# Keys of a 448-token attention in chunks of 3 x 128 + 64 instead of 4 x 112, in a fused attention and two-layer kernel

## Chip, cores and metric

The kernel runs on one core of one Trainium2 chip. The metric is the device time of one execution in microseconds; the time before is the median of three runs.

## What is computed

There are 8 batches of 12 heads with 448 tokens of 64 elements. The attention has a sigmoid in place of a softmax; behind it stand two matrix products with h - tanh(h) between them. The weights arrive as 64-bit floats.

```python
scores = matmul(q, k.transpose(0, 1, 3, 2)) / sqrt(64) - log(448)
attn = 1.0 / (1.0 + exp(-scores))
x = matmul(attn, v).transpose(0, 2, 1, 3).reshape(8 * 448, 768)
h = x @ w_in              # w_in 768 x 2048
g = h - tanh(h)
out = g @ w_out           # w_out 2048 x 768
```

## The kernel before, in words

Two heads make a pair, six pairs a batch. The transposed K and Q of a pair lie with head 0 in partitions 0 to 63 and head 1 in 64 to 127. Keys are worked off in four chunks of `CK` = 112. A chunk's scores (`scores`, L357) are matmuls with K as the weights, 64 rows and 112 columns of TensorE's array for each head, so that the heads use the two halves of its rows; each writes its own PSUM bank of the tile `sc`. Then ACT takes the sigmoid of both heads in one instruction of 112 x 896 (`weigh`, L376). AV (`av`, L386) has V's 64 columns as the weights and 112 rows, so that the heads use the two halves of the array's columns and write the two halves of the partitions of one bank, `acc`.

From batch 2 on (`AV32` = 2) everything runs in pairs of fp16 numbers, a high and a low part, and three products stand for one: six matmuls per chunk and pair for the scores, six for AV. The attention weights are split by ACT and DVE (`split_a`, L382 and L383, tile `ahl`), V by DVE (`prep_v`). Batch 1 has split scores and fp32 AV (`av32`). Batch 0 is fp32 throughout (`attention32`), its K and Q transposed by TensorE.

Tokens are loaded as `(p c)`: partition p holds tokens 4p to 4p+3, chunk c is the tokens that are c modulo 4. Each of K and Q comes in one DMA per head, V of both heads in one. For batches 1 to 7 the split K and Q (tile `w`, one buffer) are transposed by a DMA that SP issues (L343). `norms` squares K, Q and V on ACT (L308) for the scale factors. The stores of the second layer (`store` in `moe2`) undo the order of tokens, and cut a tile of 128 tokens in two where it crosses a chunk.

The stream of attention work (`stream`, pairs g = 0 to 41 of batches 1 to 7) is cut into 84 blocks of two chunks each: the first of a pair has chunks 0 and 1, the AV of the whole pair before and the next loads; the second has chunks 2 and 3 and the `norms` three pairs ahead. Seven preparing steps run within the first layer of batch 0, four blocks in `first`, and the rest within the second layer (`moe2`) of the batch before, at steps that tables set (`BLOCKS0` with 9 blocks, `BLOCKS1` with 14, `BLOCKS` with 12; 48 steps and a remainder per batch, one step being one slice f of the hidden units). The order on TensorE (PE), ACT, DVE and POOL is the order in which the code is written; only SP's order of DMAs is set by the scheduler.

During the attention of batch 0 the weights w_in come in as 24 `raw` pieces (`conv_load`, L131), are turned from 64 to 32 bits on ACT and DVE (L146 to L168), and share the queue of SP with K, Q and V. After them come the 32 `rawo` pieces of w_out, between which the stream's first loads stand.

Of the kernel before, what the change touches and what calls it, by code (L numbers as in the profile page):

```python
# [34 lines left out]
class Builder:  # L35
# [266 lines left out]
    def norms(self, loaded):  # L302

        n = len(loaded)
        ss = self.sm.tile([CK, 3], F32, name="ss", bufs=3)
        for i, t in enumerate(loaded):
            junk = self.sm.tile([CK, 8 * D], BF16, name="sqn", tag="sq", bufs=4)
            self.nc.scalar.activation(junk, t.rearrange("p a b d -> p (a b d)"), AF.Square, accum_out=ss[:, i : i + 1])  # L308
        return ss[:, :n]

    def scales(self, ss):
# [3 lines left out]
        pb = self.ps.tile([P, 512], F32, name="pbn", tag="tr", bufs=1)[:, :n]  # L315
        nc.tensor.matmul(pb, self.onesf[:CK, :], ss, start=True, stop=True)
        t = self.sm.tile([P, 3], F32, name="tn")
# [30 lines left out]
    def prep_v(self, vn, s):  # L348
        nc = self.nc
        flat = vn.rearrange("p h c d -> p (h c d)")  # L350
        v = self.att.tile([CK, 2, 2, 4, D], F16, name="vhl", tag="vhl", bufs=3)
        vf = v.rearrange("p x h c d -> p x (h c d)")
        nc.vector.tensor_scalar(vf[:, 0], flat, s[:CK, 2:3], None, op0=ALU.mult)
        nc.vector.scalar_tensor_tensor(vf[:, 1], flat, s[:CK, 2:3], vf[:, 0], op0=ALU.mult, op1=ALU.subtract)
        return v

    def scores(self, c, K, Q):  # L357

        nc = self.nc
        S = self.S  # L360
        cs = slice(c * CK, (c + 1) * CK)
# [10 lines left out]
    def weigh(self, ps, scale):  # L372
        nc = self.nc
        S = self.S
        a = self.tp.tile([CK, 2, S], F32, name="a32", tag="t")
        nc.scalar.activation(a, ps[:CK, :, :S], AF.Sigmoid, bias=self.nls[:CK], scale=scale)  # L376
        return a

    def split_a(self, a):
        nc = self.nc  # L380
        A = self.tp.tile([CK, 2, 2, self.S], F16, name="ahl", tag="t")
        nc.scalar.activation(A[:, 0], a, AF.Copy, scale=A_SCALE)  # L382
        nc.vector.scalar_tensor_tensor(A[:, 1], a, A_SCALE, A[:, 0], op0=ALU.mult, op1=ALU.subtract)  # L383
        return A

    def av(self, c, acc, v, A):  # L386
        nc = self.nc
        prods = ((0, 0), (1, 0), (0, 1))
# [10 lines left out]
    def av32(self, c, acc, vn, a):  # L399
        for h in range(2):  # L400
            self.nc.tensor.matmul(
                acc[h * D : (h + 1) * D, : self.S], vn[:, h, c, :], a[:, h], start=(c == 0), stop=(c == 3)
            )

# [29 lines left out]
    def stream(self):  # L434
# [33 lines left out]
        def prep_v(g):  # L468
            if g >= G:
                return  # L470
            if splits(g):
                vv[g] = self.prep_v(v.pop(g), sc[g][0])
            else:
                vv[g] = self.load_v(*at(g), self.att, "vhl", 3)

# [18 lines left out]
        def do_av():  # L494
            for g, c, A in todo:
                if c == 0:
                    self.acc = self.ps.tile([P, 512], F32, name="acc", tag="av", bufs=1)
                    if g % NP == 0:
                        self.xs = []
                (self.av if splits(g) else self.av32)(c, self.acc, vv[g], A)  # L500
                if c == 3:
# [5 lines left out]
        for g in range(G):  # L507
            for i in range(2):
                if i:
                    scales(g + 2)  # L510
                pss = [self.scores(c, K[g], Q[g]) for c in (2 * i, 2 * i + 1)]
                aa = [self.weigh(pss[0], sc[g][1][:CK, 0:1])]
                if i:
                    parts_k(g + 2)
                elif g:
                    parts_q(g + 1)
                aa.append(self.weigh(pss[1], sc[g][1][:CK, 0:1]))
                if i == 0 or not splits(g):
# [16 lines left out]
    def attention32(self, b, weights, rest):  # L535
# [14 lines left out]
        def prep(j):  # L550
            out = []
            for n, name in ((0, "K"), (1, "Q")):
# [4 lines left out]
                else:  # L557
                    nc.vector.tensor_copy(o, t)
                out.append(o)
            return out  # L560

        def av():
            j, c, a = todo.pop(0)
            if c == 0:
                self.acc = self.ps.tile([P, 512], F32, name="acc", tag="mm", bufs=2)
            self.av32(c, self.acc, loaded[j][2], a)
            if c == 3:
                xs.append(self.evac_x(j, self.acc, None))
# [4 lines left out]
        for j in range(NP):  # L573
            for c in range(4):
                ps = self.ps.tile([P, 2, 512], F32, name="sc", tag="sc", bufs=2)
                for h in range(2):
                    r = slice(h * D, (h + 1) * D)
                    nc.tensor.matmul(
                        ps[:CK, h, :S], qk[j][0][r, c * CK : (c + 1) * CK], qk[j][1][r], start=True, stop=True
                    )  # L580
                todo.append((j, c, self.weigh(ps, 1.0 / math.sqrt(D))))
                if j == 0 and c < 2:
# [187 lines left out]
    def moe2(self, b, gs):  # L770
# [6 lines left out]
        base = b * S  # L777
        rows = self.out[base : base + S].rearrange("(p c) e -> p c e", c=4)
        prods = ((0, 0), (0, 1), (1, 0))
        last = (self.NF - 1, 2)  # L780

        def store(o, j0, n, cols):

            i = 0
            while i < n:
                c, p = divmod(j0 + i, CK)
                k = min(n - i, CK - p)
                nc.sync.dma_start(rows[p : p + k, c, cols], o[i : i + k])
                i += k

# [57 lines left out]
    def build(self):  # L848
# [138 lines left out]
```

## Time and profile before

| what | value |
|---|---|
| runs | 1244.72 us median, 1244.56 to 1246.42 |
| profiled execution, span from first to last instruction | 1247.9 us |
| PE busy, matmuls | 1202.3 us, x7675 |
| DVE busy / ACT busy | 941.6 / 942.0 us |
| DMA | 89.76 MB, 192317 packets |

Of the profiled execution the page gives the span alone, no time of its own beside it; the span lies above all three runs. The tenths of busy time in 40 slices show PE at 9 in nearly every slice behind the ninth (a slice is 31 us), and at 7 to 9 before; the granted clock is 9 tenths or more throughout. A wait is put down to the instruction that came last, and idle time of an engine other than PE costs nothing by itself.

### The profile page before, as it was taken

The numbers are of one execution on the slowest core, as the hardware profiler recorded it, in microseconds if no ns is written. First come the engines' busy times: TensorE is split into PE (matmuls) and PEld (weight loads), VectorE is DVE, ScalarE is ACT, GpSimd is POOL, SyncE is SP. The second block draws the span as 40 slices with busy tenths as digits, with TensorE's granted clock in tenths as the row PEclk, the third lists the DMA queues.
The fourth block names the chain that finished last, engine by engine and source line by source line (L and its number), as shares of the span: only waits on it lengthen the run. The fifth ranks groups of instructions, "written<-read, shape, count | busy, mean of one in ns | idle before, by whom it ended". The sixth has DMA issues, their size and how long they took to land.

```text
span 1247.9 us, 19830 instructions
## 1 busy us (share of the span) xinstructions
PE 1202.3 (96%) x7675; PEld 651.9 (52%) x7675; DVE 941.6 (75%) x1473; ACT 942.0 (75%) x1325; POOL 38.0 (3%) x38
## 2 busy tenths in 40 slices
PE   9889887999999999999999999999999999999998
PEld 3235433455555555555555555555555655555555
DVE  4879987888966798668976789668985789636930
ACT  5857796967998688886888788886888877864820
POOL 0100000000000000100001000000000000000000
PEclk9999989999999999999999999999999999999999
DMA  9963358220044400432034400552024410300001
GB/s 241 282 171 83 89 124 208 64 61 8 4 111 100 92 1 13 107 93 57 1 65 108 95 2 1 102 110 57 1 55 100 89 25 1 72 21 20 1 14 32
DMA packets 192317, 89.76 MB, mean 72 GB/s; under 512 B 169824, under 2 KB 182368, under 8 KB 192224
## 3 DMA queue, kind: packets, MB, share of 16 engines
q1 hardware_dynamic: 191296, 88.28, 30.4%
q8 instruction: 60, 0.98, 0.3%
q10 hardware_dynamic: 928, 0.23, 0.1%
q14 instruction: 33, 0.27, 0.1%
HBM read 58.20 MB, written 11.01 MB: 55 GB/s over the span
## 4 chain that ended last, share of the span: by engine, by line
PE 71%; DVE 11%; ACT 10%; DMA 4%; issue 3%; SPq 1%; DVEq 0%; ACTq 0%
PE ph L674 31%; PE po L796 22%; PE sc L367 6%; PE acc L391 5%; PE por L834 5%; DMA raw<-moe_w_in 2%; ACT a L376 2%; ACT ahl L382 1%; ACT sqn L308 1%; DVE ahl L383 1%; DVE m L748 1%; DVE m L762 1%; DVE m L759 1%; DVE g L659 1%; DMA K<-w 1%
## 5 line engine op out<-in xcount | busy, mean ns | idle before, releaser
L796 PE MATMUL po<-wo,g 128*128 128x384 f16 x2304 | 394.1, 327 | 7.5 <-DVE o L826 4.9
L674 PE MATMUL ph<-xhl,wi 128*128 128x448 f16 x2016 | 382.6, 352 | 0.0
L796 PEld LDWEIGHTS <-g 128*128 128x128 f16 x2304 | 220.1, 98 | 183.5 <-issue 43.4
L674 PEld LDWEIGHTS <-wi 128*128 128x128 f16 x2016 | 196.7, 98 | 185.0 <-issue 1.8
L383 DVE SCALAR_TENSOR_TENSOR ahl<-a,ahl 112x896 f16<-112x896 f32 x144 | 155.7, 1122 | 68.6 <-ACT ahl L382 68.5
L376 ACT ACTIVATE a<-sc,nls,rn 112x896 f32<-112x896 f32 x168 | 179.5, 1092 | 18.7 <-PE sc L367 18.2
L744 ACT ACTIVATE u<-ph,ih 128x896 f32<-128x896 f32 x64 | 64.4, 1006 | 91.6 <-PE ph L674 87.9
L382 ACT ACTIVATE ahl<-a 112x896 f16<-112x896 f32 x144 | 128.3, 941 | 0.1
L367 PE MATMUL sc<-Q,K 64*112 64x448 f16 x1008 | 116.2, 361 | 8.9 <-ACT a L376 7.3
L748 DVE SCALAR_TENSOR_TENSOR m<-ph,ihk,u 128x896 f32<-128x896 f32 x64 | 73.4, 1147 | 38.0 <-ACT th L746 37.7
L658 ACT ACTIVATE g<-m,Sg 128x896 f16<-128x896 f32 x64 | 66.7, 1042 | 32.7 <-DVE m L762 27.3
L391 PE MATMUL acc<-ahl,vhl 112*64 112x448 f16 x864 | 89.0, 355 | 0.8 <-DVE ahl L383 0.8
L367 PEld LDWEIGHTS <-K 64*112 64x112 f16 x1008 | 60.9, 128 | 47.5 <-issue 27.8
L341 DVE SCALAR_TENSOR_TENSOR w<-qn,sn,w 112x512 f16<-112x512 f32 x42 | 31.5, 750 | 70.5 <-ACT w L338 70.2
L762 DVE COPY_PREDICATED m<-u,th 128x896 f32<-128x896 uint32 x64 | 77.3, 1208 | 6.6
L659 DVE SCALAR_TENSOR_TENSOR g<-m,Sg,g 128x896 f16<-128x896 f32 x64 | 73.3, 1146 | 8.5 <-ACT g L658 8.4
L704 PE MATMUL ph<-x,wi 128*128 128x448 f32 x192 | 76.5, 549 | 0.0
L759 DVE SCALAR_TENSOR_TENSOR m<-q,m 128x896 f32<-128x896 f32 x64 | 70.0, 1093 | 8.3 <-ACT q L758 1.2
L749 DVE SCALAR_TENSOR_TENSOR th<-ph,ih,th 128x896 f32<-128x896 f32 x64 | 73.2, 1143 | 0.0
L761 ACT ACTIVATE u<-u,b 128x896 f32<-128x896 f32 x64 | 66.8, 1044 | 6.4 <-DVE m L748 4.4
L755 DVE SCALAR_TENSOR_TENSOR m<-q,m 128x896 f32<-128x896 f32 x64 | 69.5, 1086 | 0.0
L391 PEld LDWEIGHTS <-vhl 112*64 112x64 f16 x864 | 46.0, 110 | 40.6 <-issue 13.4
(130 smaller groups left out, 1236.3 us busy)
## 6 DMA issues: line engine op xcount, KB each, us to landing
raw<-moe_w_in SPq DMA_DIRECT2D x24, 512.0 KB, 8.3
rawo<-moe_w_out SPq DMA_DIRECT2D x32, 384.0 KB, 4.1
kn<-k SPq DMA_DIRECT2D x96, 112.0 KB, 2.8
vn<-v SPq DMA_DIRECT2D x48, 224.0 KB, 3.1
qn<-q SPq DMA_DIRECT2D x94, 112.0 KB, 2.9
out<-o SPq DMA_DIRECT2D x7, 336.0 KB, 2.7
out<-o SPq DMA_DIRECT2D x7, 288.0 KB, 2.7
out<-o SPq DMA_DIRECT2D x7, 240.0 KB, 3.2
```

Of the source, the lines that this page charges most:

```text
L367: nc.tensor.matmul(ps[:CK, h, :S], K[r, w, cs], Q[r, x, :], start=(n == 0), stop=(n == len(prods) - 1))
L376: nc.scalar.activation(a, ps[:CK, :, :S], AF.Sigmoid, bias=self.nls[:CK], scale=scale)
L382: nc.scalar.activation(A[:, 0], a, AF.Copy, scale=A_SCALE)
L383: nc.vector.scalar_tensor_tensor(A[:, 1], a, A_SCALE, A[:, 0], op0=ALU.mult, op1=ALU.subtract)
L391: nc.tensor.matmul(acc[h * D : (h + 1) * D, : self.S], v[:, w, h, c, :], A[:, x, h], start=(c == 0 and n == 0), stop=(c == 3 and n == 2),)
L659: nc.vector.scalar_tensor_tensor(g[:, 1], m, Sg, g[:, 0], op0=ALU.mult, op1=ALU.subtract)
L674: nc.tensor.matmul(ph[:, e, :S], self.wi[:, c * self.NB + k, part, e * P : (e + 1) * P], xhl[c][:, x, :], start=(i == 0), stop=(i == 3 * s ...
L704: nc.tensor.matmul(ph[:, e, :S], self.where("in", c)[:, f * P : (f + 1) * P], xs[c], start=(c == 0), stop=(c == self.NC - 1),)
L748: V.scalar_tensor_tensor(m, ps, ihk, u, op0=ALU.mult, op1=ALU.mult)
L759: V.scalar_tensor_tensor(m, q2, C2, m, op0=ALU.add, op1=ALU.mult)
L762: V.copy_predicated(m, u.bitcast(U32), th)
L796: nc.tensor.matmul(po[i][:, :H], gs[f // 2][:, x, f % 2, tk * P : (tk + 1) * P], self.wo[:, i * self.NF + f, w], start=(f == 0 and n == 0) ...
```

## The change

Tokens are loaded in natural order, `(c p)`. K and Q keep their tiles of 112 partitions (and so the transposes), but the transposed columns are now tokens 0 to 447 in order, and the keys are cut into three chunks of 128 and one of 64. For the last chunk head 0 uses rows 0 to 63 and columns 0 to 63 of the array, head 1 rows 64 to 127 and columns 64 to 127. Both heads' scores of it lie in one bank, in the two halves of the partitions, so that the sigmoid and the split of the last chunk work on 128 x 448 instead of 112 x 896. V is a tile of 128 partitions and 7 rows of 64: three chunks for each head, and the seventh with head 0's last 64 tokens in the lower half and head 1's in the upper. It comes in four DMAs instead of one. The sums of squares lie in three fixed tiles that are zeroed once, since K and Q fill 112 rows of them and V 128. Each store is one DMA. `av32` is gone into `av`, and batch 0 uses the same `scores`.

```diff
-                queue.dma_start(t[:, :, h, :], src[b, 2 * j + h].rearrange("(p c) d -> p c d", c=4))
+                queue.dma_start(t[:, :, h, :], src[b, 2 * j + h].rearrange("(c p) d -> p c d", c=4))
...
     def load_v(self, b, j, pool, tag, bufs):
-        t = pool.tile([CK, 2, 4, D], F32, name="vn", tag=tag, bufs=bufs)
-        self.nc.sync.dma_start(t, self.v[b, 2 * j : 2 * j + 2].rearrange("h (p c) d -> p h c d", c=4))
+        t = pool.tile([P, 2 * QT + 1, D], F32, name="vn", tag=tag, bufs=bufs)
+        for h in range(2):
+            src = self.v[b, 2 * j + h]
+            self.nc.sync.dma_start(
+                t[:, h * QT : (h + 1) * QT], src[: QT * P].rearrange("(c p) d -> p c d", c=QT)
+            )
+            self.nc.sync.dma_start(t[h * D : (h + 1) * D, 2 * QT], src[QT * P :])
         return t
...
     def scores(self, c, K, Q):
...
-        prods = ((0, 0), (0, 1), (1, 0))
+        prods = ((0, 0), (0, 1), (1, 0)) if K.dtype == F16 else ((0, 0),)
         for n, (w, x) in enumerate(prods):
             for h in range(2):
                 r = slice(h * D, (h + 1) * D)
+                o = ps[:, h, : self.S] if c < QT else ps[r, 0, : self.S]
                 nc.tensor.matmul(
-                    ps[:CK, h, :S], K[r, w, cs], Q[r, x, :], start=(n == 0), stop=(n == len(prods) - 1)
+                    o,
+                    K[r, w, c * P : min((c + 1) * P, self.S)],
+                    Q[r, x, :],
+                    start=(n == 0),
+                    stop=(n == len(prods) - 1),
                 )
...
+    def weigh(self, c, ps, scale):
+        n = 2 if c < QT else 1
+        a = self.tp.tile([P, 2, self.S], F32, name="a32", tag="t")[:, :n]
+        self.nc.scalar.activation(a, ps[:, :n, : self.S], AF.Sigmoid, bias=self.nls, scale=scale)
...
+        n = a.shape[1]
+        A = self.tp.tile([P, 2, 2, self.S], F16, name="ahl", tag="t")[:, :, :n]
...
     def av(self, c, acc, v, A):
...
             for h in range(2):
-                nc.tensor.matmul(
-                    acc[h * D : (h + 1) * D, : self.S],
-                    v[:, w, h, c, :],
-                    A[:, x, h],
+                o = slice(h * D, (h + 1) * D)
+                k, j, i = (slice(0, P), h * QT + c, h) if c < QT else (o, 2 * QT, 0)
+                self.nc.tensor.matmul(
+                    acc[o, : self.S],
+                    v[k, w, j],
+                    A[k, x, i],
                     start=(c == 0 and n == 0),
-                    stop=(c == 3 and n == 2),
+                    stop=(c == QT and n == len(prods) - 1),
                 )
...
-                nc.sync.dma_start(rows[p : p + k, c, cols], o[i : i + k])
-                i += k
+            nc.sync.dma_start(self.out[base + j0 : base + j0 + n, cols], o)
...
+        self.sums = [const(f"ss{i}", 0.0, 3) for i in range(3)]
```

The written order on PE, ACT, DVE and POOL stays; shapes change in it. The first place is ACT in the second block of a pair (chunks 2 and 3) of a batch with split AV: `a` are the sigmoids, `ahl` the halves, `sqn` the squares of `norms`. Before:

```order
L376 ACTIVATE a_9856<-sc,nls,rn 112x896
L376 ACTIVATE a_9863<-sc,nls,rn 112x896
L382 ACTIVATE ahl<-a_9856 112x896
L382 ACTIVATE ahl<-a_9863 112x896
L308 ACTIVATE sqn,ss<-kn 112x512
L308 ACTIVATE sqn,ss<-qn 112x512
L308 ACTIVATE sqn,ss<-vn 112x512
```

With the change:

```order
L386 ACTIVATE a_9934<-sc,nls,rn 128x896
L386 ACTIVATE a_9941<-sc,nls,rn 128x448
L393 ACTIVATE ahl<-a_9934 128x896
L393 ACTIVATE ahl<-a_9941 128x448
L316 ACTIVATE sqn,ss_116<-kn 112x512
L316 ACTIVATE sqn,ss_116<-qn 112x512
L316 ACTIVATE sqn,ss_116<-vn 128x448
```

Nothing moved there; the second sigmoid and the second half have half the columns.

The second place is SP near the end of batch 0's attention, up to the last `raw` and what follows it: `raw` are pieces of w_in, `rawo` of w_out, `kn` and `qn` the first loads of the stream. Before:

```order
L286 DMA kn<-k 112x4x64
L131 DMA raw<-moe_w_in 128x512
L286 DMA kn<-k 112x4x64
L286 DMA qn<-q 112x4x64
L131 DMA raw<-moe_w_in 128x512
L131 DMA rawo<-moe_w_out 128x384
L286 DMA qn<-q 112x4x64
L131 DMA raw<-moe_w_in 128x512 x3
L286 DMA kn<-k 112x4x64 x2
L131 DMA rawo<-moe_w_out 128x384
L131 DMA raw<-moe_w_in 128x512
L286 DMA qn<-q 112x4x64 x2
```

With the change, from V of the last pair on:

```order
L294 DMA vn<-v 128x3x64
L297 DMA vn<-v 64x64
L294 DMA vn<-v 128x3x64
L297 DMA vn<-v 64x64
L131 DMA raw<-moe_w_in 128x512 x8
L131 DMA rawo<-moe_w_out 128x384
L131 DMA raw<-moe_w_in 128x512
L131 DMA rawo<-moe_w_out 128x384 x2
L286 DMA kn<-k 112x4x64 x2
L286 DMA qn<-q 112x4x64 x2
L286 DMA kn<-k 112x4x64 x2
L286 DMA qn<-q 112x4x64 x2
```

V's four issues stand together. Six of the eight K and Q loads of batch 1's first two pairs have moved behind the last `raw`, and so have two `rawo` (of the three before it then, one stands further up than these rows).

## Rows read from the trace of the kernel before

**Rows 1.** The page of the whole execution, section 1: engine, busy us, share of the span.

```profile
PE 1202.3 (96%) x7675; PEld 651.9 (52%) x7675; DVE 941.6 (75%) x1473; ACT 942.0 (75%) x1325; POOL 38.0 (3%) x38
```

**Rows 2.** The chain of waits, whole span: start us, us, engine, tile, line.

```profile
39.86 9.43 DMA raw<-moe_w_in
51.98 10.61 DMA raw<-moe_w_in
...
664.26 1.27 PE sc L367 x12
665.53 2.39 PE acc L391 x24
667.92 4.01 PE po L796 x24
...
711.42 54.59 PE ph L674 x288
766.01 7.80 PE po L796 x48
...
842.82 4.02 PE por L834 x48
...
850.50 3.90 PE por L834 x48
```

**Rows 3.** Waits of PE from 262 us on: total us, times, longest.

```profile
PE po L796 <- DVE o L826: 4.9, 6, 1.3
PE po L796 <- ACT o L825: 2.3, 3, 1.3
...
PE acc L391 <- DVE ahl L383: 0.8, 2, 0.5
```

**Rows 4.** Waits of PE from 150 to 262 us.

```profile
PE sc L367 <- ACT a L376: 7.3, 5, 2.5
```

**Rows 5.** Groups by line and shape, weight loads: busy us, mean ns, idle before.

```profile
L796 PEld LDWEIGHTS <-g 128*128 128x128 f16 x2304 | 220.1, 98 | 183.5 <-issue 43.4 <-ACT q L758 0.3
...
L367 PEld LDWEIGHTS <-K 64*112 64x112 f16 x1008 | 60.9, 128 | 47.5 <-issue 27.8 <-DMA out<-o 0.3
L391 PEld LDWEIGHTS <-vhl 112*64 112x64 f16 x864 | 46.0, 110 | 40.6 <-issue 13.4
```

**Rows 6.** Groups by line and shape, ACT and DVE.

```profile
L376 ACT ACTIVATE a<-sc,nls,rn 112x896 f32<-112x896 f32 x168 | 179.5, 1092 | 18.7 <-PE sc L367 18.2
L383 DVE SCALAR_TENSOR_TENSOR ahl<-a,ahl 112x896 f16<-112x896 f32 x144 | 155.7, 1122 | 68.6 <-ACT ahl L382 68.5
L382 ACT ACTIVATE ahl<-a 112x896 f16<-112x896 f32 x144 | 128.3, 941 | 0.1
...
L624 DVE SCALAR_TENSOR_TENSOR xhl<-x,Sx,xhl 128x448 f16<-128x448 f32 x42 | 28.7, 684 | 1.5
...
L422 ACT ACTIVATE x<-x 128x448 f32<-128x448 f32 x40 | 23.1, 576 | 2.4
L413 ACT ACTIVATE x<-acc,rn 128x448 f32<-128x448 f32 x36 | 22.8, 633 | 8.4 <-PE acc L391 5.6 <-DVE xhl L624 2.1
```

**Rows 7.** Four stretches: length, busy us per engine, PE clock, DMA share, GB/s.

```profile
28.00:74.00 46.00, 38.76 (x185) 12.39 (x184) 39.63 (x64) 36.63 (x55) 5.46 (x4) 1.00 1.08 280
230.00:262.00 32.00, 28.43 (x179) 15.21 (x178) 24.08 (x58) 31.82 (x66) 1.14 (x1) 1.00 0.31 70
514.50:515.20 0.70, 0.70 (x6) 0.43 (x5) 0.00 (x0) 0.70 (x2) 0.70 (x1) 1.00 0.78 154
541.60:545.40 3.80, 3.80 (x30) 2.37 (x29) 3.69 (x9) 2.22 (x4) 0.13 (x1) 1.00 0.46 121
```

**Rows 8.** What SP issues from 36 to 46 us: start us, us.

```profile
37.16 0.57 SPq L286 DMA_DIRECT2D kn<-k  x1
...
41.77 0.33 SPq L292 DMA_DIRECT2D vn<-v  x1
```

**Rows 9.** Waits of SP, the whole span.

```profile
SPq L343 <- DVE w L341: 427.4, 30, 62.4
```

More of the change, by code (lines that the diff above doesn't have):

```diff
@@ L304, in norms @@
         n = len(loaded)
-        ss = self.sm.tile([CK, 3], F32, name="ss", bufs=3)
+        ss = self.sums.pop(0)
+        self.sums.append(ss)
         for i, t in enumerate(loaded):
-            junk = self.sm.tile([CK, 8 * D], BF16, name="sqn", tag="sq", bufs=4)
-            self.nc.scalar.activation(junk, t.rearrange("p a b d -> p (a b d)"), AF.Square, accum_out=ss[:, i : i + 1])
+            flat = t.rearrange("p a b d -> p (a b d)" if i < 2 else "p a d -> p (a d)")
+            rows, size = flat.shape
+            junk = self.sm.tile([P, 8 * D], BF16, name="sqn", tag="sq", bufs=4)
+            self.nc.scalar.activation(junk[:rows, :size], flat, AF.Square, accum_out=ss[:rows, i : i + 1])
         return ss[:, :n]
@@ L315, in scales @@
         pb = self.ps.tile([P, 512], F32, name="pbn", tag="tr", bufs=1)[:, :n]
-        nc.tensor.matmul(pb, self.onesf[:CK, :], ss, start=True, stop=True)
+        nc.tensor.matmul(pb, self.onesf, ss, start=True, stop=True)
         t = self.sm.tile([P, 3], F32, name="tn")
@@ L349, in prep_v @@
         nc = self.nc
[L350 to L354, printed above, removed]
+        flat = vn.rearrange("p c d -> p (c d)")
+        v = self.att.tile([P, 2, 2 * QT + 1, D], F16, name="vhl", tag="vhl", bufs=3)
+        vf = v.rearrange("p x c d -> p x (c d)")
+        nc.vector.tensor_scalar(vf[:, 0], flat, s[:, 2:3], None, op0=ALU.mult)
+        nc.vector.scalar_tensor_tensor(vf[:, 1], flat, s[:, 2:3], vf[:, 0], op0=ALU.mult, op1=ALU.subtract)
         return v
@@ L380, in split_a @@
         nc = self.nc
-        A = self.tp.tile([CK, 2, 2, self.S], F16, name="ahl", tag="t")
+        n = a.shape[1]
+        A = self.tp.tile([P, 2, 2, self.S], F16, name="ahl", tag="t")[:, :, :n]
         nc.scalar.activation(A[:, 0], a, AF.Copy, scale=A_SCALE)
@@ L386, in av @@
     def av(self, c, acc, v, A):
-        nc = self.nc
-        prods = ((0, 0), (1, 0), (0, 1))
+        prods = ((0, 0), (1, 0), (0, 1)) if A.dtype == F16 else ((0, 0),)
         for n, (w, x) in enumerate(prods):
             for h in range(2):
-                nc.tensor.matmul(
-                    acc[h * D : (h + 1) * D, : self.S],
-                    v[:, w, h, c, :],
-                    A[:, x, h],
+                o = slice(h * D, (h + 1) * D)
[4 more added lines that the diff above has]
+                    A[k, x, i],
                     start=(c == 0 and n == 0),
-                    stop=(c == 3 and n == 2),
+                    stop=(c == QT and n == len(prods) - 1),
                 )
[L399 to L403, printed above, removed]
     def evac_x(self, j, acc, iv):
@@ L473, in prep_v @@
             else:
-                vv[g] = self.load_v(*at(g), self.att, "vhl", 3)
+                vv[g] = self.load_v(*at(g), self.att, "vhl", 3)[:, None]
         load(0)
@@ L499, in do_av @@
                         self.xs = []
-                (self.av if splits(g) else self.av32)(c, self.acc, vv[g], A)
+                if not splits(g):
+                    A = A[:, None]
+                self.av(c, self.acc, vv[g], A)
                 if c == 3:
@@ L511, in stream @@
                 pss = [self.scores(c, K[g], Q[g]) for c in (2 * i, 2 * i + 1)]
-                aa = [self.weigh(pss[0], sc[g][1][:CK, 0:1])]
+                aa = [self.weigh(2 * i, pss[0], sc[g][1][:, 0:1])]
                 if i:
@@ L516, in stream @@
                     parts_q(g + 1)
-                aa.append(self.weigh(pss[1], sc[g][1][:CK, 0:1]))
+                aa.append(self.weigh(2 * i + 1, pss[1], sc[g][1][:, 0:1]))
                 if i == 0 or not splits(g):
@@ L558, in prep @@
                     nc.vector.tensor_copy(o, t)
-                out.append(o)
+                out.append(o[:, None])
             return out
@@ L565, in av @@
                 self.acc = self.ps.tile([P, 512], F32, name="acc", tag="mm", bufs=2)
-            self.av32(c, self.acc, loaded[j][2], a)
+            self.av(c, self.acc, loaded[j][2][:, None], a[:, None])
             if c == 3:
@@ L574, in attention32 @@
             for c in range(4):
[L575 to L581, printed above, removed]
+                ps = self.scores(c, *qk[j])
+                todo.append((j, c, self.weigh(c, ps, 1.0 / math.sqrt(D))))
                 if j == 0 and c < 2:
@@ L777, in moe2 @@
         base = b * S
-        rows = self.out[base : base + S].rearrange("(p c) e -> p c e", c=4)
         prods = ((0, 0), (0, 1), (1, 0))
```

11 lines of the change are left out of this document (removed).

## The prediction, written before the changed kernel ran

> **What bounds the kernel now.** I read the page first, then PE's waits, then the chain of waits, then stretches. PE is busy for 1202.3 of 1247.9 us; DVE and ACT stand at three quarters [rows 1]. So time goes out only where PE waits, or where PE itself is given more or less to do. The chain shows what PE does from about 360 us on: rounds of `po` products, scores and AV products, each step released by the one before it on PE [rows 2]. In these rounds shorter ACT and DVE work is worth nothing.
>
> PE's waits say where the rest is. From 262 us to the end they are few: `po` waits 4.9 us for DVE's copy at L826 in 6 places, 1.3 us at the longest for ACT's copy at L825, and AV waits 0.8 us for `ahl` [rows 3]: 7.0 us. Between 150 and 262 us the scores wait 7.3 us for ACT's sigmoid [rows 4], and ACT is busy for 31.82 of the 32 us after 230 [rows 7]. Before 75 us the chain hangs on `raw` pieces of w_in, three landings of 9.4 to 10.6 us, of which the first and the longest stand in the rows [rows 2], at a DMA share of 1.08 and 280 GB/s [rows 7].
>
> **PE's products.** The number of matmuls stays 48 per pair of heads, and they already run two at a time. 288 `ph` products take 54.59 us, 0.1895 each; 24 AV products take 2.39 us, which is 12 x 0.1895 = 2.274 and 0.116 over [rows 2]. Both heads' products therefore pass in one product's time, for halves of the array's columns (AV) and, with 1.27 us for 12, for halves of its rows (scores). Two 64x64 corners use other rows and other columns, so I take them to overlap as well: no gain and no loss per pair.
>
> **Changes of the array's division.** What is new is that a block of scores and a pair's AV go from halves to corners in the middle. The price of such a change is in the rows. A step of scores costs 1.27 - 6 x 0.1895 = 0.133 us over its products; AV 0.116; 24 `po` products at 7.80/48 = 0.1625 take 3.90 and cost 4.01, so 0.11; `por` after scores 4.02, but after AV, which divides the array in the same way, 3.90 [rows 2]. So the overhead belongs to the change of division, and it is there when only the rows' division changes (scores to `po`) or only the columns' (AV to `po`). Going from 64x128 to 64x64, and from 128x64 to 64x64, are changes of one of the two. The corners' weights have 64 columns as AV's have, so I take AV's 0.116. There are 36 pairs of the batches that split AV (g 6 to 41), two changes each: 72 x 0.116 = **+8.4 us**, nearly all on PE's path. Ends: 0, if such a change were free, and 72 x 0.133 = 9.6. The six pairs of batch 1 add 12 changes, 1.4 us, hidden by ACT between 150 and 262 us; without that cover they would count too. In the first batch scores and AV alternate pair by pair, so each product there is behind a change already.
>
> **Weight loads.** Scores now load 128 columns of K where it was 112. The rows' loads of 112 columns last 128 ns, of 64 columns 110, of a full 128 columns 98 [rows 5], and the three overheads above stand in the same order: 0.133, 0.116, 0.11. If the loads of 64x128 behave as those of 128x128, which is the nearest row, each of the 72 steps of scores enters for 0.11 instead of 0.133: **-1.7 us**. The other end is 0.
>
> **ACT and DVE.** The last chunk is one row of 448 for both heads instead of two. ACT's sigmoid of 896 takes 1092 ns; a row of 448 read from PSUM takes 633. The half `ahl` on ACT goes from 941 to about 576 (448 from SBUF), on DVE from 1122 to 684 [rows 6]. Per split pair that is 0.46 + 0.37 = 0.83 us on ACT and 0.44 on DVE; V's squares and its two halves lose an eighth, below 0.1 each. Most of it is worth nothing, by the first paragraph. Where it counts: the first block in a batch's second layer has chunks 2 and 3 (13, 27, 39 and so on blocks of scores lie before it, an odd number), it is due at step 8 of `BLOCKS` (4 of `BLOCKS1`), and the copies L825 and L826 stand at step 16. The six waits for L826 are 0.8 us in the mean, so 0.83 on ACT and 0.44 on DVE should end most of the 7.0: I take **-6**, ends -3 and -7.0. Between 150 and 262 us six chunks lose 0.46 each [rows 6], 2.8 at most; ACT is not the bound all the way, so **-2.2**, ends -1 and -2.8.
>
> **Loads.** V comes in four DMAs of 256-byte rows instead of one of 1 KB rows. A stretch with Q loads alone moves 154 GB/s at a share of 0.78, so 197 at a full one; a stretch with V moves 121 at 0.46, so 263 [rows 7]. 224 KB take 1.16 us at the first rate and 0.87 at the second: +0.3 us, six times before 75 us, +1.8. SP needs 0.33 us to issue V now and 0.57 for a K load [rows 8]; four issues cost at most 2.3, so some 1.5 us more stands before the next `raw`. Against that, the order on SP puts six K and Q loads of the next batch (0.69 MB, 3.5 us at 197 GB/s) and two `rawo` (0.79 MB, 2.8 us at 280) behind the last `raw`, where they stood before it. DMA alone would give 1.8 - 6.3 = -4.5; but DVE is busy for 39.63 of the 46 us from 28 to 74 [rows 7], and SP's added time goes against it. I take **-1.5**, ends -4.5 and +3 (two of the six V loads exposed in SP's issue time). Later, V's issues stand on SP before the K transposes, but these wait for DVE's `w` in any case, 427.4 us in all [rows 9]. Stores become fewer and nobody waits for them. Three memsets stand on DVE ahead of its first copy of K, which waits for K's landing in any case.
>
> **Sum.** 8.4 - 1.7 - 6 - 2.2 - 1.5 = -3.0 us. The profiled execution spans 1247.9 us, 3.2 above the median of the three runs, 1244.72; against its own span the change would give 1244.9, against the median **1241.7**. A measurement of this kernel tells 0.2%, 2.5 us, from no change, so this is faster by hardly more than that.
>
> **Rivals.**
> First, slower: the relief does not come back. PE's waits for L826 are ended by DVE's order, in which `o` stands behind two `ahl`; only the block's second `ahl` gets shorter, and in half of the blocks none does. For it: ACT's queue is full there and something else may take its place. Against it: in the mean the six waits are no longer than what ACT alone loses. If none of the 7.0 and half of the 2.2 returns, the sum is 8.4 - 1.7 - 1.1 - 1.5 = +4.1, and +5.6 if the first 75 us give nothing: about 1250. It decides as soon as less than 3 us of the 6 return. Chance 0.20.
> Second, slower: the corners do not overlap. Both corners of a chunk write one PSUM bank, from different rows of the array. Scores' halves write two banks, AV's halves one bank from the same rows, so no row shows this case. Each of 6 pairs of products would cost 0.1895 more: 36 x 6 x 0.1895 = 41 us, so about 1283. Against it: they write different partitions, as AV's halves do. Chance 0.09. The Trainium skill, TensorEngine Tiling (Array Packing), section Restrictions and Gotchas, says that different row tiles cannot access the same PSUM bank at the same time; it speaks for this rival, and no run here shows it yet.
> Third, faster: halves to corners is no change that costs, since one of the two divisions stays. Without the 8.4 it is 1233. Against it: the 0.11 of AV to `po`, where the rows' division stays too. Chance 0.08. The same page, section Tiling Modes, says that changing the tiling mode, not just the tile, drains TensorE; by that the 8.4 stays.
> Fourth, slower: the loads. The single buffer `w` is free for ACT and DVE only after its transpose on SP, and V's 1.5 us on SP stand before it; or `raw` falls behind by that much for four of the pairs, +6 in the first 75 us instead of -1.5: about 1249. Chance 0.13.
>
> **Numbers.** The forecast has 0.50; by its ends it lies between 1236 and 1249, likely 1238 to 1246. The range 1235 to 1252 takes in the first and fourth rivals and leaves out the second (0.09), most of the third and the tails, 0.2 in all. Faster by over 0.2% (below 1242.2): 0.32 of the forecast's half, the third rival, a little of the first: 0.42. Within 0.2%: 0.22. Slower: 0.36.
>
> **What would show it.** A step of scores with chunks 2 and 3 should last about 1.36 us on the chain, one with chunks 0 and 1 1.25, and 24 AV products 2.5; 1.9 and 3.1 would mean corners one after the other. The waits of `po` for L826 should fall below 2 us. The last `raw` should land before 74 us. If these hold and the time is still not lower, the sizes are wrong and not the steps; if V's loads show up in waits of ACT for `w`, the fourth rival holds.

## The result, and the profile after

| | median us | range, runs | ratio to before, 95% interval |
|---|---|---|---|
| before, beside the changed kernel | 1245.40 | 1243.34 to 1247.11, 6 | 1 |
| changed kernel | 1249.78 | 1249.59 to 1252.35, 6 | 1.0038 [1.0027, 1.0050] |

It is slower by 0.38%, 4.7 us; the forecast was 3.0 us faster. The ratio is one of means; the medians differ by 4.4 us. The profiled execution has a span of 1250.0 us and took 1252.35 us, the longest of its six; a time is about 2.3 us over its span here.

The page, section 1 of the changed kernel (before: [rows 1]):

```profile
PE 1209.4 (97%) x7675; PEld 627.3 (50%) x7675; DVE 920.4 (74%) x1476; ACT 910.7 (73%) x1325; POOL 37.8 (3%) x38
```

DVE and ACT lost 21 and 31 us of work, PE gained 7.1. The chain of waits in the changed kernel (before: [rows 2]; L374 is `scores`, L405 `av`):

```profile
415.50 4.02 PE por L832 x48
419.53 1.24 PE sc L374 x12
420.77 2.51 PE acc L405 x24
423.28 4.02 PE por L832 x48
...
489.80 1.36 PE sc L374 x12
491.16 4.01 PE po L794 x24
495.17 1.24 PE sc L374 x12
```

Scores with chunks 0 and 1 take 1.24 us, with chunks 2 and 3 1.36; AV 2.51 where it took 2.39; `por` after AV 4.02 where it took 3.90. PE's waits from 262 us to the end (before: [rows 3]):

```profile
PE po L794 <- DVE o L824: 2.6, 2, 1.3
PE po L794 <- ACT o L823: 2.2, 4, 1.0
PE por L832 <- ACT o L823: 1.1, 2, 0.6
PE acc L405 <- DVE ahl L394: 0.4, 1, 0.4
```

The waits for DVE's copy fell from six to two; the two left are as long as the longest before. The prediction's sign, less than 2 us, is missed with 2.6. Weight loads by shape (before: [rows 5]):

```profile
L374 PEld LDWEIGHTS <-K 64*128 64x128 f16 x756 | 30.4, 94 | 45.8 <-issue 22.2 <-DMA rawo<-moe_w_out 3.0 <-DMA vn<-v 0.7
...
L374 PEld LDWEIGHTS <-K 64*64 64x64 f16 x252 | 10.9, 106 | 20.8 <-issue 17.1 <-DVE iK L780 0.4
L405 PEld LDWEIGHTS <-vhl 64*64 64x64 f16 x216 | 8.9, 105 | 15.6 <-issue 12.7
```

And what SP issues from 34 to 42 us, in the first batch (before: [rows 8]; here start, us, and the number of issues):

```profile
35.36 2.69 SPq L294 DMA_DIRECT2D vn<-v  x1
38.10 1.20 SPq L297 DMA_DIRECT2D vn<-v  x1
39.35 0.58 SPq L294 DMA_DIRECT2D vn<-v  x1
39.98 0.49 SPq L297 DMA_DIRECT2D vn<-v  x1
40.58 1.76 SPq L131 DMA_DIRECT2D raw<-moe_w_in  x3
```

V holds SP for 5.1 us, and the next `raw` is issued behind it. The first 2.1 of them are a wait for PE's `sc`, and the four issues take the other 3.0. The chain shows this as well, from 0 to 80 us:

```profile
14.48 1.16 SPq L294
15.69 1.31 SPq L297
17.04 0.59 SPq L294
17.67 0.49 SPq L297
18.21 4.30 DMA raw<-moe_w_in
...
30.40 4.40 DMA raw<-moe_w_in
...
36.43 0.99 PE sc L374 x4
37.43 0.62 SPq L294
...
40.58 4.76 DMA raw<-moe_w_in
```

So the delay goes round: a landing of `raw` is late, ACT and then PE's scores come later behind it, V's issues wait for those scores, and the next `raw` stands behind V.

For where time goes, the first layer of each batch is a good mark: its 288 `ph` products stand on the chain in one row per batch. For the changed kernel, batches 1, 2 and 7:

```profile
274.86 54.60 PE ph L679 x288
427.30 54.59 PE ph L679 x288
...
1134.35 54.59 PE ph L679 x288
```

The table gives the time to the first of these rows, from the first to the second, and from the second to the last (five batches, 30 pairs of heads), each from such rows of that kernel's chain. E1 to E12 are the experiments below.

| kernel | to batch 1 | batch 1 to 2 | batch 2 to 7 |
|---|---|---|---|
| before, as profiled for the prediction | 276.07 | 151.69 | 704.29 |
| before again (E12) | 270.01 | 151.66 | 703.89 |
| changed kernel | 274.86 | 152.44 | 707.05 |
| E1, whole array in the last chunk | 272.00 | 150.26 | 702.75 |
| E2, the same for scores alone | 273.90 | 152.37 | 704.12 |
| E3, the same for AV alone | 274.01 | 150.28 | 703.05 |
| E4, last chunk at full width on ACT and DVE | 275.99 | 152.65 | 708.20 |
| E5, batch 0 as before | 270.98 | 150.71 | 706.84 |
| E6, natural order only | 269.59 | 150.14 | 704.16 |
| E7, E1 with Q's cuts late | 275.19 | 154.20 | 702.38 |
| E8, before with Q's cuts late | 273.68 | 152.23 | 706.12 |
| E9, batch 0 in 112s, one V transfer | 268.51 | 152.47 | 706.63 |
| E10, E9 with E1's last chunk | 268.28 | 151.98 | 702.83 |
| E11, E6 with four V transfers | 272.04 | 151.82 | 704.23 |

The last column hardly scatters: four pieces of 112 keys give 703.9 to 704.3, corners 706.6 to 707.1, whichever first batch goes with them. The first column differs by 6.06 us between the two profiles of the kernel before; there the medians decide. The second is the same in these two, but over the kernels it falls into two groups: E1, E3, E5 and E6 have 150.1 to 150.7 us at a mean granted clock of 1.00, the others 151.7 to 154.2 at 0.98 or 0.99. In E12 the clock falls to 0.50 from 356 to 358 us, after 2 us in which PE, waiting for the late copies, was busy for 0.32; in E6 it stays at 1.00 behind much the same waits. So about 1.5 us of this column are the clock of one execution.

### The profile page after: what moved, and what is told of

Read it like the earlier page. It is cut to its first block, busy times and chain, and to the rows that moved or that the text cites. A ratio compares the mean times of both kernels' runs of the same rounds, so it can differ in the third digit from the quotient of the medians.

```text
span 1250.0 us, 20037 instructions
## 1 busy us (share of the span) xinstructions
PE 1209.4 (97%) x7675; PEld 627.3 (50%) x7675; DVE 920.4 (74%) x1476; ACT 910.7 (73%) x1325; POOL 37.8 (3%) x38
## 4 chain that ended last, share of the span: by engine, by line
PE 79%; ACT 7%; DVE 7%; DMA 3%; issue 2%; SPq 1%; DVEq 0%; ACTq 0%
PE ph L679 31%; PE po L794 26%; PE sc L374 7%; PE acc L405 7%; PE por L832 5%; PE ph L709 2%; ACT a L386 2%; DMA raw<-moe_w_in 1%; ACT wo L215 1%; DMA qn<-q 1%; DVE g L664 1%; DVE m L753 1%; DVE m L767 1%; DVE wo L218 1%; DVE m L764 1%
## 5 line engine op out<-in xcount | busy, mean ns | idle before, releaser
L394 DVE SCALAR_TENSOR_TENSOR ahl<-a,ahl 128x896 f16<-128x896 f32 (+1 forms) x144 | 138.8, 1004 | 71.2 <-ACT ahl L393 71.2
L386 ACT ACTIVATE a<-sc,nls,rn 128x896 f32<-128x896 f32 (+1 forms) x168 | 163.5, 997 | 36.3 <-PE sc L374 34.4
L374 PE MATMUL sc<-Q,K 64*128 64x448 f16 x1008 | 116.7, 356 | 8.8 <-ACT a L386 6.9
L393 ACT ACTIVATE ahl<-a 128x896 f16<-128x896 f32 (+1 forms) x144 | 114.7, 846 | 0.4 <-DVE n_y L98 0.4
L405 PE MATMUL acc<-ahl,vhl 128*64 128x448 f16 (+1 forms) x864 | 93.0, 356 | 0.4 <-DVE ahl L394 0.4
L663 ACT ACTIVATE g<-m,Sg 128x896 f16<-128x896 f32 x64 | 66.6, 1041 | 34.0 <-DVE m L767 28.7
L764 DVE SCALAR_TENSOR_TENSOR m<-q,m 128x896 f32<-128x896 f32 x64 | 69.9, 1093 | 9.9 <-ACT q L763 2.2
L374 PEld LDWEIGHTS <-K 64*128 64x128 f16 x1008 | 41.3, 97 | 66.5 <-issue 39.3
L405 PEld LDWEIGHTS <-vhl 128*64 128x64 f16 (+1 forms) x864 | 42.7, 108 | 48.7 <-issue 26.7
```

The lines of the kernel that those rows point to most:

```text
L374: nc.tensor.matmul(o, K[r, w, c * P : min((c + 1) * P, self.S)], Q[r, x, :], start=(n == 0), stop=(n == len(prods) - 1),)
L386: self.nc.scalar.activation(a, ps[:, :n, : self.S], AF.Sigmoid, bias=self.nls, scale=scale)
L405: self.nc.tensor.matmul(acc[o, : self.S], v[k, w, j], A[k, x, i], start=(c == 0 and n == 0), stop=(c == QT and n == len(prods) - 1),)
L764: V.scalar_tensor_tensor(m, q2, C2, m, op0=ALU.add, op1=ALU.mult)
```

## The experiments

Theory A: the loss is the changes of the array's division, and the shorter work on ACT and DVE did not make up for them. Theory B: the loads of the first batch cost.

| | median us | before beside it | ratio, 95% interval |
|---|---|---|---|
| E1 | 1244.55 | 1243.53 | 1.0006 [0.9998, 1.0015] |
| E2 | 1245.98 | 1243.53 | 1.0021 [1.0012, 1.0030] |
| E3 | 1244.77 | 1243.53 | 1.0009 [1.0000, 1.0017] |
| E4 | 1251.13 | 1243.53 | 1.0065 [1.0052, 1.0077] |
| E5 | 1246.74 | 1244.43 | 1.0021 [1.0011, 1.0031] |
| E6 | 1241.68 | 1244.43 | 0.9983 [0.9974, 0.9992] |
| E7 | 1249.19 | 1244.43 | 1.0039 [1.0027, 1.0051] |
| E8 | 1248.67 | 1244.43 | 1.0035 [1.0023, 1.0047] |
| E9 | 1245.49 | 1243.86 | 1.0013 [1.0003, 1.0022] |
| E10 | 1241.35 | 1243.86 | 0.9984 [0.9975, 0.9993] |
| E11 | 1246.13 | 1243.86 | 1.0016 [1.0007, 1.0026] |
| E12 | 1243.67 | 1243.86 | one run |

### E1 to E3: no new change of division

The last chunk uses the whole array: K's two corners are copied by POOL into a 128x128 tile with zeros beside them, V's last rows are loaded into such a tile. Three products do what six did. E2 does this for the scores alone, E3 for AV alone.

```diff
+            if kd is not None and c == QT:
+                nc.tensor.matmul(ps[:, 0, : self.S], kd[:, w], Q[:, x, :], start=(n == 0), stop=(n == len(prods) - 1))
+                continue
...
+            if c == QT and A.dtype == F16:
+                self.nc.tensor.matmul(
+                    acc[:, : self.S], v[:, w, 2 * QT :].rearrange("p c d -> p (c d)"), A[:, x, 0], start=False, stop=(n == len(prods) - 1)
+                )
+                continue
```

> The changed kernel, with the last chunk of a pair as one product for both heads on the whole array in place of two corners: the weights are K's (or V's) two 64x64 blocks on the diagonal of 128x128 and zeros beside them, copied by POOL for K (42 pairs of copies) and zeroed by POOL in V's tile. Scores and AV of the 36 pairs with split AV then change the array's division as often as the kernel before did, while ACT and DVE keep the short last chunk. Theory A, the extra changes of division cost what the rows of the kernel before gave (72 x 0.116 us): 8.4 us faster than the changed kernel, about 1241.4, and so 4 us faster than the kernel before. Theory B, the loss comes from elsewhere (V's loads in small rows, SP's order, the corners' own products): within 2 us of the changed kernel, 1248 to 1252. In the chain a step of scores with chunks 2 and 3 should last 1.36 under B and 1.24 to 1.25 under A.

> The changed kernel with only the scores' last chunk as one product on the whole array; AV keeps its corners. Theory A: half of the extra changes go, 36 x 0.116 = 4.2 us, about 1245.6, the time of the kernel before. Theory B: 1248 to 1252.

> The changed kernel with only AV's last chunk as one product on the whole array; the scores keep their corners. Theory A: 4.2 us, about 1245.6. Theory B: 1248 to 1252.

Without the corners 0.32% comes back, 4.0 us, about half of 8.4. Of that 0.5 lies outside the span: a time is 1.8 us over its span in E1, E2, E3, E7 and E10, and 2.3 in most other kernels, which was not followed. The five batches show why it is not more. They last 4.3 us less than with corners, but the waits between these marks (first the changed kernel, then E1) grew again:

```profile
PE po L794 <- DVE o L824: 1.3, 1, 1.3
PE por L832 <- ACT o L823: 0.5, 1, 0.5
PE po L794 <- ACT o L823: 0.2, 1, 0.2
```

```profile
PE po L816 <- DVE o L846: 2.8, 5, 1.3
PE por L854 <- ACT o L845: 0.5, 1, 0.5
```

PE's own work fell by 4.3 + 1.3 = 5.6 us for 60 changes, 0.093 each; the forecast had 0.116. The step of scores with chunks 2 and 3 did not fall to 1.24 or 1.25, as theory A had put its sign; in E1 it is two rows with the change between them, 1.35 us together, and it is `po` behind it that pays nothing, 3.90 where it took 4.01:

```profile
511.34 0.67 PE sc L389 x6
512.02 0.67 PE sc L384 x3
512.69 3.90 PE po L816 x24
```

E2 and E3 save 2.9 and 4.0 of the 707.05; together they would be 6.9, and both at once gave 4.3. The waits part them. Beside 0.5 of `por` E2 has the first row below, and E3 has `por` alone:

```profile
PE po L808 <- DVE o L838: 1.4, 5, 0.3
```

```profile
PE por L840 <- ACT o L831: 0.5, 1, 0.5
```

With these taken off, PE's own work fell by 2.8 and 2.5, together 5.3, near E1's 5.6: the work adds, and the waits do not. So the changes cost, as theory A says, and in E1 a part of what is taken from PE turns into waits for ACT and DVE. E1 was still not faster than before, so A is not all.

### E4: the relief taken away

The sigmoid and the two halves of the last chunk keep their old width; the second half of the result is not used.

```diff
-        n = 2 if c < QT else 1
-        a = self.tp.tile([P, 2, self.S], F32, name="a32", tag="t")[:, :n]
-        self.nc.scalar.activation(a, ps[:, :n, : self.S], AF.Sigmoid, bias=self.nls, scale=scale)
+        a = self.tp.tile([P, 2, self.S], F32, name="a32", tag="t")
+        src = ps[:, :, : self.S] if c < QT else ps[:, 0:1, : self.S].to_broadcast([P, 2, self.S])
+        self.nc.scalar.activation(a, src, AF.Sigmoid, bias=self.nls, scale=scale)
```

> The changed kernel with sigmoid, split and low half of the last chunk at 896 columns again, the second 448 a repetition of the first that nobody reads; TensorE's work and the loads stay. Shows what the shorter ACT and DVE work is worth. If it came back as PE's waits say (7.0 us from 262 us on before, 4.0 after, and some 1 us ahead of it): 4 us slower than the changed kernel, about 1254. If the shorter work is hidden everywhere: 1249 to 1251. If it was worth what was forecast (8.2): about 1258.

The ratio rises from 1.0038 to 1.0065: the relief is worth some 3.4 us in all, by the two intervals give or take 2, and 1.15 in the five batches. In those, E4 waits

```profile
PE po L794 <- DVE o L824: 2.4, 5, 1.3
```

where the kernel before waited 3.6 us in five places (four of 0.6, one of 1.3). The waits are shorter although the sigmoids and splits are as wide as before: PE itself now comes later, by the changes. About half of what the four short waits gave back was taken by PE's longer steps, half by the relief, and the long one stood in all three kernels. Ahead of batch 1, from 75 to 276 us, the scores wait 8.2 us for the sigmoid in E4, 6.9 in the changed kernel, and all of PE's waits there are 22.5 and 20.6: the relief is worth 1.3 to 1.9 us there, by one execution of each.

### E5, E6, E9, E11: the first batch

E5 is the changed kernel with batch 0 as before (tokens in the order `(p c)`, pieces of 112, V of both heads in one transfer), E9 the same in the natural order; E6 is the kernel before with the natural order alone (`(c p)` for K and Q, `h (c p) d` for V in one transfer, one store per tile), E11 is E6 with V of batch 0 issued in four transfers per pair. In `load_v` of E5:

```diff
+        if b == 0:
+            t = pool.tile([CK, 2, 4, D], F32, name="vn", tag=tag, bufs=bufs)
+            self.nc.sync.dma_start(t, self.v[b, 2 * j : 2 * j + 2].rearrange("h (p c) d -> p h c d", c=4))
+            return t
```

E9 reads `h (c p) d` there. E11 against E6:

```diff
+        if b:
+            self.nc.sync.dma_start(t, self.v[b, 2 * j : 2 * j + 2].rearrange("h (c p) d -> p h c d", c=4))
+        else:
+            for h in range(2):
+                src = self.v[b, 2 * j + h]
+                self.nc.sync.dma_start(t[:, h, :3], src[: 3 * CK].rearrange("(c p) d -> p c d", c=3))
+                self.nc.sync.dma_start(t[:, h, 3], src[3 * CK :])
-        self.nc.sync.dma_start(t, self.v[b, 2 * j : 2 * j + 2].rearrange("h (c p) d -> p h c d", c=4))
```

> The changed kernel with its first batch alone put back as in the kernel before: keys and queries in four pieces of 112 tokens, V of both heads in one transfer, the old order of stores; all later batches in corners. Theory B (the first batch's loads cost: V's four issues hold SP for 5 to 6 us each, and the raw weights stand behind them) expects 2 to 4 us less than the changed kernel, a ratio to the kernel before of 1.001 to 1.002, the first stream matmul of batch 0 back within 0.5 us of 70.1 us, and no V issue on the chain of waits before 75 us. Theory A (all of the loss is changes of the array's division after 276 us) expects the changed kernel's time, 1.0038 within 0.001.

> The kernel before with the natural order of tokens alone: four pieces of 112 keys stay, K, Q and V are read in 256-byte rows (V of both heads still in one transfer), the stores go out in one transfer per tile. Nothing of the array's work changes. Theory B in its wide form (short rows in the first batch cost, whoever issues them) expects 1 to 3 us more than the kernel before, all of it ahead of the first stream matmul of batch 1 (276.0 us before). Theory B in its narrow form (what costs is V's four issues on SP) expects the kernel before's time within 0.8 us (0.9994 to 1.0006), as Theory A does.

> The changed kernel with the first batch alone on four pieces of 112 keys and V of both heads in one transfer, in the natural order of tokens. Theory D: the change has three parts, an order that gives 2 us back in the first batch's loads (experiment 6), V's four issues and short pieces in the first batch that cost 3 to 4 us, and the corners in the later batches that cost 3 to 3.5 us; they add. It expects 1.0005 to 1.0015 times the kernel before, 3 to 4 us less than the changed kernel. Theory A expects the changed kernel's 1.0038 (the first batch does not matter).

> Experiment 6 (the kernel before in natural order) with one more edit: V of the first batch goes out in four transfers per pair (each head's first 336 rows and its last 112), as the changed kernel issues it; the tiles and all work on them stay. Theory D expects that these four issues cost 3 to 4 us: 1.0005 to 1.0015 times the kernel before, where experiment 6 had 0.9983. If it is the 64-key pieces and the array's work in the first batch that cost there, 0.9983 to 0.9990.

The natural order alone is a gain that neither theory had: 0.17%, 2.1 us, none of it behind batch 2. Four V transfers instead of one take it away and more: 0.9983 to 1.0016, 4.1 us, with the same array work. In the two profiles 2.45 of that lie ahead of batch 1 and 1.68 between batches 1 and 2, where E11's clock falls to 0.50 at 358 us and E6's does not; over all 11 executions of each the mean granted clock is the same (0.9936 and 0.9934), so nothing says that the clock parts the medians. With corners in the later batches, V in one transfer and pieces of 112 in the first batch are worth 1.0038 - 1.0013, 3.1 us (E9), and 2.1 us in the old order (E5). So theory B holds in its narrow form for V, and within the intervals the three parts add as theory D has it. Some signs were missed: E5's 1.0021 and E11's 1.0016 lie just above what was expected, and E5's first `ph` product of batch 0 stands at 66.6 us and not near 70.1, with one issue of V on its chain, at 2.4 us. SP in E11, from 32 us on:

```profile
32.63 2.71 SPq L297 DMA_DIRECT2D vn<-v  x1
...
37.05 0.47 SPq L298 DMA_DIRECT2D vn<-v  x1
37.63 2.83 SPq L131 DMA_DIRECT2D raw<-moe_w_in  x4
```

It is the changed kernel's picture (four issues, then `raw`), and E11's chain up to 80 us has five landings of `raw`, of 4.0 to 8.5 us. E6 has a single one:

```profile
44.14 5.47 DMA raw<-moe_w_in
```

Otherwise E6's chain runs through DVE, PE and ACT there. E11 does not part SP's time from the smaller transfers themselves; that V's issues stand on its chain from 13.90 us on, with `raw` behind them, speaks for SP. Why the natural order itself gains (256-byte rows, the order in which SP then comes to issue the loads, or the stores) was not separated; `raw` lands in 6.0 us in the median in E6 and in 7.3 in E12.

### E7 and E8: ACT's wait for the transposed K

E1's chain before a late copy runs through K's transpose into ACT's cut of Q:

```profile
489.94 2.99 DMA K<-w
...
493.04 0.72 ACT w L349
493.76 0.98 ACT a L401
```

Theory C was that ACT, done sooner, only waits for this transfer, and that the relief is lost there. The edit moves the cut behind the second sigmoid, in E1 (E7) and in the kernel before (E8).

```diff
                 if i:
                     parts_k(g + 2)
-                elif g:
+                aa.append(self.weigh(2 * i + 1, pss[1], sc[g][1][:, 0:1]))
+                if g and i == 0:
                     parts_q(g + 1)
-                aa.append(self.weigh(2 * i + 1, pss[1], sc[g][1][:, 0:1]))
```

> The kernel of experiment 1 (no change of the array's division in the last chunk: block-diagonal weights on the whole array) with one more edit: ACT's two cuts of Q for the next pair stand behind the second sigmoid of the block, not ahead of it. Theory C (the shorter sigmoids gave little back because ACT stands in front of these cuts until the transpose of K has freed the single buffer w, so that the sigmoid behind it starts when it did before) expects 2 to 3.5 us less than experiment 1, and TensorE's waits for DVE's evictions (o) at 0.5 us or less where experiment 1 has 4.2 us. If ACT's wait was covered, as theory A has it, the time is experiment 1's within 1 us.

> The kernel before with the same single move of ACT's cuts of Q behind the second sigmoid, nothing else. Theory C expects that the order on ACT was worth 1 to 3 us in the kernel before as well: 1241 to 1243 us on the scale where it takes 1244, with TensorE's waits for DVE's o from 4.9 us to about 3. If the wait for w is covered by other work, no difference within 0.8 us.

Theory C's forecast fails: both are slower, by 4.1 us (E7 against E1) and 4.4 us (E8 against before). In the five batches E7 still waits 2.7 us in five places (E1: 2.8); E8 waits longer than the kernel before, 5.9 us against 3.6:

```profile
PE po L796 <- DVE o L826: 5.9, 5, 1.2
```

The edit does not take the wait out alone, though. DVE's part of the cut and its split of V stand behind ACT's cut and move with it. In E1 DVE is idle for 1.02 us ahead of its two `ahl` in front of the copy; in E7 it goes from the split of V into them without a gap, and the copy L846 starts 76.85 us behind the mark of batch 2 where E1 has 76.77. In batch 4, where E1 has the long wait, it starts at 77.10 instead of 77.93, and the longest wait falls from 1.3 to 0.7. E7 loses most of its time ahead of batch 2; between the marks of batches 1 and 2 PE waits 5.1 us where E1 waits 3.6, and the rest was not followed.

So E7 does not settle theory C, but the traces of the kernel before and the changed kernel do, for these places. ACT's cut of Q in batch 2, before and with the change:

```profile
498.83 0.73 ACT L338 ACTIVATE w<-qn,sn 112x512 f16<-112x512 f32 x1
```

```profile
498.01 0.72 ACT L346 ACTIVATE w<-qn,sn 112x512 f16<-112x512 f32 x1 [0.34 <-DMA K<-w]
```

Counted from the batch's mark (427.76 and 427.30 us), ACT's sigmoid ahead of this cut starts 0.82 us sooner with the change, the cut and DVE's copy only 0.36. The rest goes into waiting for the transposed K, whose transfer follows DVE's cut of K, and that ends at the same distance from the mark in both (67.5 us). PE comes 0.25 us later; 0.36 and 0.25 are the short wait of 0.6 that went. Batches 3, 5 and 6 show the same within 0.04 us. In batch 4 the transfer lasts longer than E1's 2.99 us above, and it stands on the chain of the changed kernel:

```profile
779.61 4.53 DMA K<-w
```

ACT is idle for 1.86 us ahead of the cut there, where it was for 0.75 before, and the copy comes 0.30 us later from the mark than before: the wait of 1.3 stays. In E2 and E3 ACT waits for K there for 0.42 and 0.27 us, and the long wait is gone. Why this one transfer is slow was not followed. SP issued it 67.6 us behind the mark in both kernels, so V's issues did not hold it up.

### E10 and E12

E10 is E9 with the whole array of E1. E12 is the kernel before, unchanged, for a second profile.

> Experiment 9 with the block-diagonal weights of experiment 1 in the later batches. Theory D expects both gains to add: 0.996 to 0.998 times the kernel before, at or under the natural order alone (0.9983), so the fastest of all these. If the first batch's gain is eaten by what follows it, 1.0000 to 1.0006.

> The kernel before itself, for a second profile. The profiled execution from which the prediction was made had a span of 1247.9 us, some 5 us above what its median execution leaves for a span. Theory D expects that this lay ahead of the first stream matmul of batch 2: from there to the last matmul the same 815.4 us within 0.3, and the first stream matmul of batch 1 before 274.5 us rather than at 276.0.

E10 misses its forecast: 0.9984 where 0.996 to 0.998 was expected, beside 0.9983 for E6. It is 2.0 us under the kernel before and 6.7 under the changed one, as E6 is, and E6 is far simpler. Against E9 the whole array gives 3.6 us; against four pieces of 112 it gives nothing that the medians show, though its five batches last 1.3 us less than E6's.

E12 on the marks:

```profile
270.01 54.60 PE ph L674 x288
421.67 54.60 PE ph L674 x288
```

Batch 1 starts 6.06 us earlier than in the profile that the prediction was made from, and the rest is the same within 0.5 us. Of landings of `raw` its chain has two, 9.21 and 9.15 us, not three.

## Why the prediction was wrong, step by step

**Bound.** Right: PE is the bound, and only its waits and its own work count. DVE and ACT lost 52 us between them, and the kernel is slower.

**Corners overlap.** Right: chunk steps of 1.36 and AV of 2.51 us, where 1.9 and 3.1 would have meant one after the other. The second rival is out; the rule of the Trainium skill that it cited (TensorEngine Tiling (Array Packing), Restrictions and Gotchas: different row tiles cannot access one PSUM bank at the same time) cost no time in this form, and the measurement decides.

**Changes of division, +8.4, and weight loads, -1.7.** Right in mechanism and near in size, a little too dear. 128 columns load in 94 ns where 112 took 128 [rows 5], and the step with chunks 0 and 1 fell from 1.27 to 1.24. Overlooked: AV now ends in corners, so `por` behind it pays as well, 0.12 once per batch. Batch 2 to 7, PE's own work went from 704.29 - 4.1 (waits of 3.6 and 0.5) to 707.05 - 2.0, so by 4.9 us for 30 pairs; the prediction's terms give (8.4 - 1.7) x 30/36 = 5.6. The third rival is out: the corners cost.

**Relief on ACT and DVE, -6.** This step failed. It took the shortened block with chunks 2 and 3, the first in the second layer, set ACT's 0.83 us less against the mean wait of 0.8 at L826, and concluded that most of the 7.0 would go. Between that block and the copy stands one with chunks 0 and 1, whose sigmoids and splits keep their length, and in it ACT's cut of Q waits for the transposed K. The prediction passed over this wait. Of the 0.82 us by which ACT is sooner, 0.36 reach the copy in four batches and nothing in batch 4 (E7 and E8). The mean also hid two kinds: four waits of 0.6 went; two of 1.3, the first ahead of batch 2 and one ahead of batch 5, stayed as they were, and the waits for ACT's copy, 2.3 before, are 2.2. From 262 us on the waits of `po`, `por` and `acc` went from 9.1 (the three in [rows 3] and 1.1 of `por`; the 7.0 had counted the longest of ACT's copy instead of its 2.3) to 6.3: 2.8 came back. By E4, about half of what the short waits gave back in the five batches went to PE's longer steps, so the same microsecond was counted as a cost of PE and as a gain of ACT. From batch 1 on E4's marks leave 1.4 us to the relief (1.15 and 0.2), where 6 were taken. This is the first rival's condition, less than 3 us returned.

**Relief from 150 to 262 us, -2.2.** Near, as far as single executions show: E4 puts 1.3 to 1.9 us on it. Against the kernel before it does not show in the wait it was read from: from 75 to 276 us the scores' wait for the sigmoid is 6.9 us where it was 7.3, and PE's wait for the converted weights (`stb`) is 10.3 where it was 8.4; a wait of 2.2 for `rawo` is gone, and all together are 20.6 where they were 22.5.

**Loads, -1.5.** Failed in both parts, +2.0 by E11. V's issues were priced at SP's issue time, at most 2.3 us for four; they held SP for 3.7 us at 14.48 us and, with the wait for PE's scores, for 5.1 at 35.36, and the next `raw` stood behind them; in the two kernels with four transfers the chain has four and five landings of `raw` up to 80 us, in E6 one. V's pieces cost 4.1 us (E11 against E6), where the transfers were priced at 1.8 in all and SP's time was only set against the gain. The six loads and two `rawo` behind the last `raw`, -6.3 by the DMA's rates, are not seen as such a gain; what the natural order gives is 2.1 us. The last `raw` did land before 74 us, and that showed nothing, because the landings of 9.4 to 10.6 us [rows 2] were those of a long execution: ACT turns the last piece at 73.7 us in the changed kernel, at 69.9 in E12.

**The base.** The profile before was 3.2 us above the median by its span, and by a time 2.3 us over that span about 5.5; E12 places all of it ahead of batch 1, in the stretch where the loads were judged.

**Sum.** Corners in the later batches: +2.8 to 3.2 from batch 2 to 7 and +0.8 from 1 to 2, some 3.7 us. First batch, V's four transfers +4.1, order -2.1. Together 5.7 where 4.7 is measured, with intervals of 1.1 to 1.5 us either way on each ratio. Against the forecast of -3.0 the two large misses are the relief (-8.2 taken, about -3 found) and the loads (-1.5 taken, +2.0 found). The time lies in the range, on the side that had 0.36; it is the first rival with a part of the fourth (`raw` behind V). That the first rival's about 1250 is met so closely is partly luck: its sum has 1.1 us of relief and 0 to 1.5 gained on the loads, where about 3 and a loss of 2.0 were found.

## What to carry to other kernels

Take a group of waits apart by place before setting a saving against its mean, follow the saved time through every step up to the wait (here one stood behind a transfer that did not move), and remember that work added to the waiting engine eats the same wait: it can be counted once. A transfer cut in four is priced by how long it holds its queue, waits included, and by what stands behind it there, not by its bytes. Two profiles of the kernel before, at least for a stage that loads, are worth more than a close reading of one.

## What the runs showed of the hardware that was not expected

A late `raw` can cost more than its lateness. In the changed kernel `sc` waits 2.4 us for ACT around 34 us, and the granted clock falls behind that (windows of 2 us; the columns are those of [rows 7]):

```profile
34.00:36.00 2.00, 0.02 (x2) 0.00 (x0) 0.45 (x2) 1.18 (x2) 0.00 (x0) 1.00 0.95 328
36.00:38.00 2.00, 1.57 (x6) 0.49 (x8) 1.93 (x3) 2.00 (x5) 1.07 (x1) 0.84 1.00 383
38.00:40.00 2.00, 1.78 (x6) 0.50 (x4) 1.97 (x3) 2.00 (x4) 0.39 (x1) 0.50 1.24 264
40.00:42.00 2.00, 2.00 (x12) 0.30 (x8) 1.90 (x5) 0.33 (x1) 0.00 (x0) 0.80 1.03 158
```

PE was idle from 34 to 36 us, ran at 0.50, the lower level of 1.2 GHz, from 38 to 40, and was back at full clock at 42: (0.16 + 0.50 + 0.20) x 2 = 1.7 us of clock lost at most. How much of it reached the time is not shown, since ACT was busy throughout from 36 to 40 us. In the long profile of the kernel before the same stands at 78 to 82 us, at 0.62 and 0.53, behind waits of 2.0 us for ACT; E6, E9 and E12 have 1.00 from 28 to 100 us, and so has E11, for all its late `raw`. So a part of the scatter of the first 276 us between executions may be the clock. And a weight load of 64 rows with 128 columns took 94 ns, less than one with 64 columns, 106.
